# A sliding-window attention block on one core: E by V in tiles of 64 by 32, five equal score sets, masks by VectorE, layer norm as multiply and add

## The chip, the cores and the metric

The kernel runs on one core of one Trainium2 chip. The time is device microseconds of one execution: the median of three runs of the kernel before is 323.15 us (322.97 to 323.19).

## The reference

One transformer block over 2048 positions of width 640, in bfloat16. A vector `c` gives six modulation vectors (shift, scale and gate for each half of the block). With `x` of 2048 by 640:

```python
sa, ca, ga, sb, cb, gb = (silu(c) @ w_mod) split in six
h = layernorm(x) * (1 + ca) + sa
q, k, v = h @ wqkv, in 32 heads of 20
p = softmax(q @ k.T / sqrt(20), only keys with 0 <= query - key < 256)
x = x + ga * ((p @ v) @ wo)
h = layernorm(x) * (1 + cb) + sb
x = x + gb * ((sigmoid(h @ w_gate) * (h @ w_up)) @ w_down)
```

Each query sees 256 keys: itself and the 255 before it. The inner width of the second half is 1536.

## The kernel before, in words

The 2048 positions are cut in eight chunks of 256 queries (two blocks of 128). For each chunk `a` the work is: layer norm and modulation (`ln1`), projection to q, k and v (`qkv`), attention in two halves of 16 heads (`attention`, `q` = 0 and 1, called half chunks here), output projection and residual (`outproj`), second layer norm, gated MLP (`mlp`). A chunk's queries need the keys of two blocks before it and of its own two; chunk 0 has no keys before it.

**Order of the work.** `build` only collects operations with their readers, writers and buffers. `PLAN` (line 365) is a list written out beforehand: each number divided by 5 is an operation, and the remainder is the engine that runs it (0 TensorE, 1 ScalarE, 2 VectorE, 3 GpSimd, here POOL as in the profile, 4 SyncE). `schedule` (line 151) walks this list, places tiles in buffers and keeps each engine's order; `emit` (line 262) works out the semaphore waits. Every engine runs its own operations strictly in that order. [...] The chunks overlap: the projections run ahead of attention, and the MLP of earlier chunks fills TensorE between the pieces of attention.

**Scores.** q and k stand transposed in `QT` and `KT`, four heads on the four groups of 32 partitions (20 used). For chunks 1 to 7 a half chunk has four main sets and one ends set. A main set (`main_set`, line 1052) is 24 matmuls in tiles of 32 rows by 64 columns, eight at once: keys in groups of 64, over the pieces of queries that `PIECES` lists (256, 192 and 64 queries). They fill the four banks of `S`; one ScalarE instruction (line 1067) takes the exponential of all 128 x 2048 into a buffer `E`. An ends set (`ends_set`, line 1027) holds the far and near corners of four heads' windows: 32 matmuls of 64 queries in tiles of 32 rows by 128 columns, one exponential (line 1041) into a buffer `G`. POOL then masks with affine selects (lines 1045, 1072, 1076), part of which copy corners from `E` to `G`. Chunk 0 has three sets for each half chunk (`score_set`, line 1082), masked on line 1112.

**E by V.** `burst` (line 1121) makes one operation for each half chunk: 64 matmuls (32 in chunk 0) in tiles of 128 rows by 32 columns. The stationary operand is 128 keys by one head's 20 values, a column of ones for the softmax sum, and padding (heads stand 22 apart in `V`); the moving operand is `E` or `G`, 256 or 128 queries. Four tiles, one for each group of 32 output partitions, work at once, and the sums go to two banks of `M` (two heads side by side in each). In chunks 1 to 7 the burst is glued ahead of the second score set of the next half chunk (`with_pv`, line 1001). Then VectorE transposes, takes the reciprocal of the sums, divides, and transposes again (lines 1162 to 1194).

**V.** For each block of 128 keys two chains of five matmuls (320 columns each, heads 0 to 15 and 16 to 31) go to a bank of `M`; one eviction each, on ScalarE or VectorE as the list says (lines 914, 915), writes `V`. `M` has four banks, which all projections, the MLP and the bursts share.

**Layer norm.** VectorE computes mean and variance (`bn_stats`, `bn_aggr`), POOL adds epsilon and raises to -0.5 (lines 800, 802), and the normalisation is subtract and multiply on VectorE (line 815); for six blocks, fixed in `XHP`, POOL does it as multiply and add (lines 807, 812).

Of the kernel before, what the change touches and what calls it, by code (L numbers as in the profile page):

```python
# [360 lines left out]
def c_pe(n):  # L361
# [133 lines left out]
FILL = 1  # L495
WSE = (("dve", "pool"), ("dve", "pool"))
QMAX = 4.5
NE = 6
EW = 2048
PAIR = 0  # L500
PAIRO = 0
XHP = ((2, 0), (3, 0), (4, 0), (4, 1), (5, 0), (5, 1))
MOE = ("dve", "act", "pool")


# [882 lines left out]
```

## Time and profile before

| | |
|---|---|
| median of three runs | 323.15 us |
| span of the profiled execution (first to last instruction) | 321.8 us |
| matmuls / weight loads | 5045 / 5045 |
| VectorE instructions | 424 |
| ScalarE instructions | 229 |
| POOL instructions | 349 |
| HBM read / written | 18.68 MB / 2.62 MB |

How to read it: the span is that of the one execution that the profiler recorded; what lies around it (323.15 - 321.8 = 1.35 us, launch and end) is part of the measured time and not of the profile. Engines are PE (TensorE matmul), PEld (TensorE weight load, which overlaps PE), DVE (VectorE), ACT (ScalarE), POOL (GpSimd) and SP. All matmuls are recorded by one helper, lines 698 (whole array) and 699 (tiles), so they are told apart by the names of their tiles: `S<-QT,KT` are scores, `M<-E,V` is E by V. A line of the timeline gives start, length, engine, line, operation, output and inputs, shape of the array tile, and the count of instructions merged in it; in brackets stands the idle time before it and what ended that. A line of the groups gives busy time, mean nanoseconds of one, and the idle time before them. A line of the stretches gives busy time and count for PE, PEld, DVE, ACT and POOL, then the granted clock and the share and rate of the DMA engines.

### The profile page before, as it was taken

The numbers are of one execution on the slowest core, as the hardware profiler recorded it, in microseconds if no ns is written. First come the engines' busy times: TensorE is split into PE (matmuls) and PEld (weight loads), VectorE is DVE, ScalarE is ACT, GpSimd is POOL, SyncE is SP. The second block draws the span as 40 slices with busy tenths as digits, with TensorE's granted clock in tenths as the row PEclk, the third lists the DMA queues.
The fourth block names the chain that finished last, engine by engine and source line by source line (L and its number), as shares of the span: only waits on it lengthen the run. The fifth ranks groups of instructions, "written<-read, shape, count | busy, mean of one in ns | idle before, by whom it ended". The sixth has DMA issues, their size and how long they took to land.

```text
span 321.8 us, 11465 instructions
## 1 busy us (share of the span) xinstructions
PE 315.6 (98%) x5045; PEld 236.8 (74%) x5045; DVE 198.8 (62%) x424; ACT 213.9 (66%) x229; POOL 189.5 (59%) x349
## 2 busy tenths in 40 slices
PE   6999999999999999999999999999999999999996
PEld 2677767677877777766777677877877777877885
DVE  4689987877886746584555555465534474386323
ACT  2699997877787986768686867676976746411220
POOL 3338759878768493949484848577575826601000
PEclk9999999999999999999999999999999999999999
DMA  7999999999922534126526100220800004002101
GB/s 249 348 262 278 223 179 248 194 225 295 206 36 43 88 75 55 44 63 108 77 19 111 37 22 2 63 42 25 132 18 4 22 22 104 20 5 61 43 0 41
DMA packets 62123, 32.92 MB, mean 102 GB/s; under 512 B 45946, under 2 KB 60794, under 8 KB 62074
## 3 DMA queue, kind: packets, MB, share of 16 engines
q1 hardware_dynamic: 59904, 29.73, 43.5%
q10 hardware_dynamic: 2170, 2.46, 2.8%
q8 instruction: 39, 0.64, 0.9%
q14 instruction: 10, 0.08, 0.1%
HBM read 18.68 MB, written 2.62 MB: 66 GB/s over the span
## 4 chain that ended last, share of the span: by engine, by line
PE 96%; DMA 1%; DVE 1%; ACT 1%; issue 0%; ACTq 0%
PE M L698 79%; PE S L699 8%; PE M L699 7%; DMA x<-in_A_x_dram 1%; ACT hT L831 1%; DVE st L793 1%; PE S L698 1%; PE S L690 0%; ACT stg L914 0%; ACTq L584 0%; DVE x L815 0%; DVE st L795 0%; ACT hT L914 0%; DVE x L1308 0%; DVE mA L778 0%
## 5 line engine op out<-in xcount | busy, mean ns | idle before, releaser
L1067 ACT ACTIVATE E<-S 128x2048 bf16<-128x2048 f32 x56 | 105.0, 1875 | 40.6 <-PE S L699 40.2
L1072 POOL TENSOR_SCALAR_AFFINE_SELECT E<-E 128x256 bf16<-128x256 bf16 x112 | 46.6, 427 | 57.1 <-ACT E L1067 25.1
L1076 POOL TENSOR_SCALAR_AFFINE_SELECT E<-E 128x512 bf16<-128x512 bf16 x112 | 70.6, 646 | 4.6 <-DVE x L815 1.2
L698 PE MATMUL M<-h2T,wg 128*128 128x256 bf16 x480 | 67.0, 273 | 0.0
L698 PE MATMUL M<-h2T,wu 128*128 128x256 bf16 x480 | 66.7, 273 | 0.0
L1289 DVE SCALAR_TENSOR_TENSOR hh<-sig,M 128x512 bf16<-128x512 f32 x48 | 32.4, 678 | 42.9 <-ACT sig L1287 26.4
L698 PE MATMUL M<-wd,hh 128*128 128x320 bf16 (+2 forms) x396 | 57.1, 295 | 0.0
L698 PEld LDWEIGHTS M<-h2T,wg 128*128 128x128 bf16 x480 | 45.4, 98 | 7.8 <-DVE T L1162 0.2
L698 PEld LDWEIGHTS M<-h2T,wu 128*128 128x128 bf16 x480 | 45.2, 98 | 7.3
L1287 ACT ACTIVATE sig<-M 128x512 f32<-128x512 f32 x48 | 28.5, 595 | 31.2 <-PE M L698 30.9
L698 PEld LDWEIGHTS M<-wd,hh 128*128 128x128 bf16 x396 | 37.2, 98 | 13.7 <-DVE hh L1289 0.2
L1045 POOL TENSOR_SCALAR_AFFINE_SELECT E<-E 128x1024 bf16<-128x1024 bf16 x28 | 32.0, 1147 | 4.9 <-ACT E L1041 3.4
L699 PEld LDWEIGHTS S<-QT,KT 20*64 20x64 bf16 (+1 forms) x1856 | 20.0, 100 | 17.4 <-issue 9.7
L699 PE MATMUL S<-QT,KT 20*64 20x256 bf16 (+5 forms) x1856 | 32.3, 228 | 0.4 <-issue 0.4
L1041 ACT ACTIVATE E<-S 128x2048 bf16<-128x2048 f32 x14 | 26.3, 1876 | 6.8 <-PE S L699 6.7
L793 DVE BATCH_NORM_STATS2 st<-x 128x6 f32<-128x320 bf16 x64 | 28.9, 479 | 2.4 <-DMA x<-in_A_x_dram 1.8
L1162 DVE STREAM_TRANSPOSE T<-M 128x512 f32<-128x512 f32 x32 | 21.5, 700 | 12.9 <-PE S L699 11.6
L698 PE MATMUL M<-wk,hT 128*128 128x320 bf16 x160 | 27.9, 299 | 0.0
L1308 DVE TENSOR_TENSOR x<-M,x 128x320 bf16<-128x320 f32 (+2 forms) x33 | 15.4, 475 | 18.8 <-PE M L698 18.6
L698 PE MATMUL M<-wq,hT 128*128 128x320 bf16 x160 | 26.2, 299 | 0.7 <-DVE hT L832 0.5
L698 PE MATMUL M<-wv,hT 128*128 128x320 bf16 x160 | 26.0, 299 | 0.0
L698 PE MATMUL M<-wo,oT 128*128 128x320 bf16 x160 | 25.9, 299 | 0.0
(84 smaller groups left out, 356.4 us busy)
## 6 DMA issues: line engine op xcount, KB each, us to landing
x<-in_A_x_dram SPq DMA_DIRECT2D x18, 160.0 KB, 3.7
wd<-in_w_mod_dram SPq DMA_DIRECT2D x6, 320.0 KB, 5.4
wd<-in_B_w_down_dram SPq DMA_DIRECT2D x4, 480.0 KB, 5.5
wu<-in_w_mod_dram SPq DMA_DIRECT2D x5, 320.0 KB, 4.8
x<-in_A_x_dram ACTq DMA_DIRECT2D x8, 160.0 KB, 2.7
out_dram<-x SPq DMA_DIRECT2D x8, 160.0 KB, 1.9
wu<-in_B_w_up_dram SPq DMA_DIRECT2D x2, 576.0 KB, 4.7
wg<-in_B_w_gate_dram SPq DMA_DIRECT2D x2, 576.0 KB, 6.8
```

The lines of the kernel that those rows point to most:

```text
L698: return e.matmul(o, l, r, start=st, stop=sp, skip_group_check=True)
L699: return e.matmul(o, l, r, start=st, stop=sp, tile_position=tp, skip_group_check=True)
L793: A("dve", lambda e, g, bi=bi, j=j: e.bn_stats(v(bi * 12 + j * 6, 6), src[bi].ap[:, j * 320:(j + 1) * 320]), 0.48, reads=[src[bi].r()], wr ...
L1041: A("act", lambda e, eng: e.activation(cell().rearrange("p m (x c) -> p m x c", c=64)[:, :, 0:4:3, :], Sp.ap[:].rearrange("p j (k x c) -> ...
L1045: A("pool", lambda e, eng, c0=c0, pat=pat, base=base, cm=cm: e.affine_select(cell()[:, :, c0:c0 + 64], cell()[:, :, c0:c0 + 64], pattern=p ...
L1067: A("act", lambda e, eng: e.activation(part(0, 512), Sp.ap[:], ACT.Exp, scale=SM_SCALE), 1.876, reads=[Sp.r()], writes=[E.r("C"), E.r("B") ...
L1072: A("pool", lambda e, eng, hc=hc, src=src, far_h=far_h: e.affine_select(side(hc), part(src, 64), pattern=[[0, 4], [-1 if far_h else 1, 64] ...
L1076: A("pool", lambda e, eng, c0=c0, near=near: e.affine_select(part(c0, 128), part(c0, 128), pattern=[[0, 4], [1 if near else -1, 128]], com ...
L1162: A("dve", lambda e, g, h=h: e.transpose(T1.ap[:, 512 * h:512 * h + 512], X[h].ap), 0.694, reads=[X[h].r()], writes=[T1.r(h)], prio=3.5, t ...
L1287: A("act", lambda e, g, pg=pg, sg=sg: e.activation(sg.ap[:], pg.ap[:], ACT.Tanh, scale=0.5), c_act(512), reads=[pg.r()], writes=[sg.r()], ...
L1289: A("dve", lambda e, g, pu=pu, sg=sg, f0=f0: e.scalar_tensor_tensor(out=hh.ap[:, f0:f0 + 2, :], in0=sg.ap[:].rearrange("p (a b) -> p a b", ...
L1308: A("dve", lambda e, g, ps=ps, bi=bi, c0=c0, n=n: e.tensor_tensor(x1[bi].ap[:, c0:c0 + n], ps.ap[:, 0:n], x1[bi].ap[:, c0:c0 + n], op=ALU. ...
```

## The change

- **Score sets.** All sets of a half chunk have one form: tiles of 32 rows by 64 columns, 512 columns for each tile, eight tiles at once. The two column halves of the array now hold two pairs of heads (before: two groups of 64 keys of the same heads). A group of 64 keys `x` (from -4 to 3, counted from the chunk's start) is scored against the 64, 128, 192 or 256 queries that can see it, so nothing is scored in both an ends set and a main set. Five sets for each half chunk: two of pieces of 256, two of 192, 64, 64, 192, one of 128. The ends set and `G` go. Chunk 0 has two sets for each half chunk and one that both share: five, where it had six.
- **E by V.** Tiles of 64 rows by 32 columns: 64 keys, eight tiles at once. The lower and upper 64 partitions hold different heads and add into different banks of `M`. 128 matmuls for each half chunk (64 in chunk 0); the lengths follow `LENS`.
- **V** is laid out to match: each projection chain of 320 columns takes every other pair of heads from `wv`, and two evictions of 64 partitions each bring it to the partitions of its heads: 64 evictions where there were 32.
- **Masks** are one VectorE minimum each (two from a set of chunk 0's first two) of `E` with a buffer `mk` that holds 0 or 3e38, the row block of `mk` repeated over the groups: 79 of them. `mk` is made once at the start.
- **Layer norm** is multiply and add for all blocks but chunk 0's first norm: POOL computes the negated mean and its product with the inverse deviation (two small operations for each norm), and the list chooses VectorE or POOL for the normalisation.
- `E` has eight buffers where it had six and `G` (the same memory). The order list is a new one, with 1977 operations where it had 2097.

```diff
-NE = 6
+NE = 8
 EW = 2048
+BIG = 3.0e38
...
+            def mki(e, g, p0=p0, c0=c0, op=op):
+                src = p_sig.aps[0][p0:p0 + 64, p0:p0 + 64].bitcast(I32)
+                for i in range(2):
+                    ins = e.tensor_scalar(mk[p0:p0 + 64, c0 + i * 64:c0 + i * 64 + 64], src, 0.0, BIG, op0=op, op1=ALU.mult)
+                return ins
...
+        if not one:
+            A("pool", lambda e, g: e.tensor_scalar(v(34, n), st.ap[:, 24:28].rearrange("p (b t) -> p b t", t=2)[:, :, 0], -1.0, None,
+                                                   op0=ALU.mult), 0.2,
...
+                return e.tensor_scalar(dst[bi].ap[:], src[bi].ap[:], v(30 + bi, 1), v(32 + bi, 1), op0=ALU.mult, op1=ALU.add)
+            A("dve" if one else ("dve", "pool"), xh, {"dve": 0.44, "pool": 0.87}, port=True,
...
+                    ps.ap[:, 0:320].rearrange("p (g c) -> p g c", c=40), hT[a].ap[:, kt, bi * 128:(bi + 1) * 128],
+                    wv[:, kt, :].rearrange("p (g c) -> p g c", c=80)[:, :, 40 * half:40 * half + 40])) for kt in range(NDT)]
...
+                for odd in range(2):
+                    evac(lambda b=b, half=half, odd=odd: heads(V[b].ap[64 * half:64 * half + 64, 352 * odd:352 * odd + 352], VW)[:, :, 0:DH],
+                         lambda ps=ps, odd=odd: heads(ps.ap[64 * odd:64 * odd + 64, 0:320], DH), 320, [ps.r()], [V[b].r((half, odd))], 6.5,
+                         f"evv{a}")
...
+    ONE = ((-1, 0), (0, 256))
+    TWO = ((-2, 0), (-4, 192), (3, 256), (1, 320))
+    SETS = (([(h, x, c) for x, c in st] for st in (ONE, TWO) for h in range(2)))
+    SETS = [list(x) for x in SETS] + [[(h, x, c + 256 * h) for h in range(2) for x, c in ((-3, 0), (2, 128))]]
+    MASKS = [(192, 512, 4, 128, 64)] * 2 + [(128, 512, 4, 256, 0)] * 2 + [(64, 256, 8, 128, 64)]
+    FIRST = ((1, 0), (3, 192), (0, 256))
...
+                v = E.ap.rearrange("p (g c) -> p g c", c=step)[:, :, c0:c0 + w]
+                return e.tensor_tensor(v, v, mk[:, m0:m0 + w].unsqueeze(1).to_broadcast([128, g, w]), op=ALU.min)
...
+    XS = {64: (-4, 3), 128: (-3, 2), 192: (-2, 1), 256: (-1, 0)}
+    LENS = (64, 256, 192, 192, 128, 128, 192, 256, 128, 128, 192, 256, 256, 64, 64, 64)
+    LENS0 = (64, 192, 256, 256, 128, 128, 192, 64)
...
+                ins = mm(e, X[half].ap[32 * j:32 * j + 32, h * 256 + q0:h * 256 + q0 + n],
+                         V[2 * a + kb].ap[64 * half:64 * half + 64, v0:v0 + 32],
+                         E.ap[64 * half:64 * half + 64, j * 512 + c:j * 512 + c + n], t not in seen, True, tp=(64 * half, 32 * j))
```

A helper, `run`, issues the matmuls of a set or a burst: it goes round the eight tiles and always takes the one whose columns so far are fewest.

More of the change, by code (lines that the diff above doesn't have):

```diff
@@ L1001, in with_pv @@
+    last = {"s": fills, "p": []}
     def with_pv(name, sc, dur, rd, tiles, before, mode):
         if before is None:
-            return A("pe", sc, dur, reads=list(rd), writes=[tiles[-1].r()], prio=10, lat=0.2, tag=name, extra=last["s"], mode=mode,
-                     hold=tiles[:-1])
+            return A("pe", sc, dur, reads=list(rd), writes=[t.r() for t in tiles[1:]], prio=10, lat=0.2, tag=name, extra=last["s"], mode=mode,
+                     hold=tiles[:1])
         pa, pv, pd, prd, X = before
@@ L1011, in with_pv @@
         rd.update(prd)
-        return A("pe", both_of, pd + 0.09 + dur, reads=list(rd), writes=[tiles[-1].r(), X[0].r(), X[1].r()], prio=10, lat=0.2,
-                 tag=f"pvs{pa}", extra=last["s"], mode=2, mout=mode, hold=tiles[:-1] + X)
+        return A("pe", both_of, pd + 0.09 + dur, reads=list(rd), writes=[t.r() for t in tiles[1:]] + [X[0].r(), X[1].r()], prio=10, lat=0.2,
+                 tag=f"pvs{pa}", extra=last["s"], mode=4, mout=mode, hold=tiles[:1] + X)
     def keys_of(a, kb, lo, gi, j, n):
@@ L1020, in set_reads @@
         rd = {}
-        for kb in range(-2, 2):
+        for kb in range(-2 if a else 0, 2):
             rd[KT[(2 * a + kb) // 2].r((kb % 2, q))] = 1
@@ L1121, in burst, with run @@
-    def burst(a, q, sets, Es, G):
+    def run(e, prog, emit):
+        at = {t: p[0] for t, p in prog.items()}
+        pos = dict.fromkeys(prog, 1)
+        ins = None
+        while pos:
+            t = min(pos, key=lambda t: (at[t], list(prog).index(t)))
+            what = prog[t][pos[t]]
+            if isinstance(what, int):
+                at[t] = max(at[t], what)
+            else:
+                ins = emit(e, t, what)
+                at[t] += what[-1]
+            pos[t] += 1
+            if pos[t] == len(prog[t]):
+                del pos[t]
+        return ins
@@ new lines, in score_set, with put, fn @@
+    def score_set(a, name, parts, masks, before):
+        E, Sp = Tile(p_E, f"E{a}_{name}"), Tile(p_S, f"S{a}_{name}")
+        def sc(e, eng):
+            prog = {(j, half): [0] + [(q, h, x, c, piece(x)[3]) for q, h, x, c in parts] for j in range(4) for half in range(2)}
+            def put(e, t, what):
+                j, half = t
+                q, h, x, c, n = what
+                kb, odd, q0, n = piece(x)
+                gi = 4 * q + 2 * half + h
+                return mm(e, Sp.ap[64 * half:64 * half + 64, j, c:c + n], keys_of(a, kb, 64 * odd, gi, j, 64),
+                          QT[a].ap[32 * j:32 * j + DH, gi, q0:q0 + n], True, True, tp=(32 * j, 64 * half))
+            return run(e, prog, put)
+        rd = {}
+        for q in dict.fromkeys(x[0] for x in parts):
+            rd.update(set_reads(a, q))
+        last["s"] = [with_pv(f"score{a}", sc, 0.262, rd, [E, Sp], before, 3)]
+        A("act", lambda e, eng: e.activation(E.ap.rearrange("p (j c) -> p j c", j=4), Sp.ap[:], ACT.Exp, scale=SM_SCALE), 1.876,
+          reads=[Sp.r()], writes=[E.r()], prio=3, tag=f"exp{a}")
+        for c0, step, g, w, m0 in masks:
+            def fn(e, eng, c0=c0, step=step, g=g, w=w, m0=m0):
+                v = E.ap.rearrange("p (g c) -> p g c", c=step)[:, :, c0:c0 + w]
+                return e.tensor_tensor(v, v, mk[:, m0:m0 + w].unsqueeze(1).to_broadcast([128, g, w]), op=ALU.min)
+            A("dve", fn, c_dve(g * w, 2.0), port=True, reads=[E.r(), R_mk], writes=[E.r()], prio=5, tag=f"mask{a}")
+        for q, h, x, c in parts:
+            where[a, q, h, x] = E, c
+        return E
@@ L1123, in burst @@
+    XS = {64: (-4, 3), 128: (-3, 2), 192: (-2, 1), 256: (-1, 0)}
+    LENS = (64, 256, 192, 192, 128, 128, 192, 256, 128, 128, 192, 256, 256, 64, 64, 64)
+    LENS0 = (64, 192, 256, 256, 128, 128, 192, 64)
+    where = {}
+    def burst(a, q):
         X = [Tile(p_M, f"O{a}_{q}x"), Tile(p_M, f"O{a}_{q}y")]
         X[0].mate, X[1].mate = X[1], X[0]
+        of = {n: [(h, x) for h in range(2) for x in XS[n] if a or x >= 0] for n in XS}
+        mine = [p + where[(a, q) + p] for p in (of[n].pop(0) for n in (LENS if a else LENS0))]
@@ L1139, in pv @@
-            for (E, _), st in zip(Es, sets) if not a else ():
-                for k, kb, u, n, cu in st[0]:
-                    bank = k // 2
-                    oc = (k % 2) * 256 + u * 128
-                    for j in range(4):
-                        h = 16 * q + 4 * j + k
-                        ins = mm(e, X[bank].ap[32 * j:32 * j + 32, oc:oc + n * 128], V[2 * a + kb].ap[:, h * VW:h * VW + 32],
-                                 E.ap[:, j * 512 + cu * 128:j * 512 + (cu + n) * 128], (bank, j) not in seen, True, tp=(0, 32 * j))
-                        seen.add((bank, j))
@@ L1154, in burst @@
+            return run(e, prog, put)
+        rd = {x[2].r(): 1 for x in mine}
         for kb in range(-2 if a else 0, 2):
-            rd[V[2 * a + kb].r(0)] = 1
-            rd[V[2 * a + kb].r(1)] = 1
-        return a, pv, (6 if a else 3) * 512 / 2400.0 * 1.04 + 0.02, rd, X
+            for half in range(2):
+                for odd in range(2):
+                    rd[V[2 * a + kb].r((half, odd))] = 1
+        return a, pv, 1.165 if a else 0.6, rd, X
     def norm(X, Tn, q, a):
@@ L1172, in build, with later @@
     pend = []
-    def later(a, q, sets, Es, G, close):
+    def later(a, q, close):
         made = []
         def first():
-            made.append(burst(a, q, sets, Es, G))
+            made.append(burst(a, q))
             return made[0]
@@ L1183, in alone @@
         pa, pv, pd, prd, X = first()
-        A("pe", pv, pd, reads=list(prd), writes=[X[0].r(), X[1].r()], prio=8, lat=0.2, tag=f"pvs{pa}", mode=2, hold=X, extra=last["s"])
+        A("pe", pv, pd, reads=list(prd), writes=[X[0].r(), X[1].r()], prio=8, lat=0.2, tag=f"pvs{pa}", mode=4, hold=X, extra=last["s"])
         then()
@@ L1215, in attention @@
             if a < NOW:
-                alone(*later(a, q, sets, Es, G, close))
+                alone(*later(a, q, close))
             else:
-                pend.append(later(a, q, sets, Es, G, close))
+                pend.append(later(a, q, close))
     def add_pair(x, pss, prio, tag):
```

195 lines of the change are left out of this document (43 added, 152 removed), and 218 rows, old and new, of the table PLAN.

## The prediction

> **What bounds the kernel now.** I read the page first, then the chain that ended last, then the busy times in stretches of 20 us, then the timeline around one burst, and last the groups by line and shape.
>
> ```profile
> span 321.8 us, 11465 instructions
> PE 315.6 (98%) x5045; PEld 236.8 (74%) x5045; DVE 198.8 (62%) x424; ACT 213.9 (66%) x229; POOL 189.5 (59%) x349
> PEclk9999999999999999999999999999999999999999
> PE 96%; DMA 1%; DVE 1%; ACT 1%; issue 0%; ACTq 0%
> PE M L698 79%; PE S L699 8%; PE M L699 7%; DMA x<-in_A_x_dram 1%; ACT hT L831 1%; DVE st L793 1%; PE S L698 1%; PE S L690 0%; ACT stg L914 0%; ACTq L584 0%; DVE x L815 0%; DVE st L795 0%; ACT hT L914 0%; DVE x L1308 0%; DVE mA L778 0%
> ```
>
> TensorE is the chain: 96% of it, at the full granted clock. No other engine is above 66%. So a microsecond less of TensorE work is a microsecond less of time, as long as nothing else makes it wait. The places where something could are the stretches in which VectorE is nearly full:
>
> ```profile
> 20.00:40.00 20.00, 20.00 (x407) 14.21 (x405) 18.81 (x47) 18.81 (x22) 15.27 (x24) 1.00 1.06 259
> 40.00:60.00 20.00, 19.60 (x332) 13.55 (x331) 16.00 (x39) 16.82 (x21) 15.02 (x28) 1.00 1.15 210
> 60.00:80.00 20.00, 20.00 (x322) 14.66 (x320) 15.45 (x34) 15.68 (x17) 16.14 (x29) 1.00 1.12 246
> 80.00:100.00 20.00, 20.00 (x348) 15.19 (x347) 16.80 (x40) 16.02 (x16) 13.55 (x24) 1.00 0.58 111
> 100.00:120.00 20.00, 20.00 (x348) 15.03 (x347) 12.20 (x26) 16.20 (x20) 14.96 (x28) 1.00 0.42 75
> ```
>
> The columns after the length are PE, PEld, DVE, ACT, POOL. From 20 to 40 us VectorE and ScalarE are each busy 18.81 of 20, and TensorE still loses nothing. From 100 us on VectorE has room: 12.20 of 20.
>
> **The change part by part.**
>
> *The burst (E by V).* Fourteen bursts of 64 matmuls (chunks 1 to 7, two each) and two of 32 (chunk 0). One of the fourteen, with the score set behind it and a later "ends" set:
>
> ```profile
> 189.19 1.30 PEld L699 LDWEIGHTS M<-E,V 128*32 128x32 bf16 x64 [0.30 <-POOL E L1076]
> 190.66 0.27 PEld L699 LDWEIGHTS S<-QT,KT 20*64 20x64 bf16 x24 [0.16 <-issue]
> 191.01 0.11 PEld L698 LDWEIGHTS M<-h2T,wg 128*128 128x128 bf16 x2
> 191.25 1.04 PE L698 MATMUL M<-h2T,wu 128*128 128x256 bf16 x8
> 192.12 0.43 PE L698 MATMUL M<-wo,oT 128*128 128x320 bf16 x2
> 192.39 0.82 PE L698 MATMUL M<-h2T,wg 128*128 128x256 bf16 x6
> 193.05 0.38 PE L698 MATMUL M<-h2T,wu 128*128 128x256 bf16 x2
> 193.36 0.29 PEld L699 LDWEIGHTS S<-QT,KT 20*128 20x128 bf16 x32 [0.21 <-issue]
> 193.70 0.25 PEld L698 LDWEIGHTS M<-wo,oT 128*128 128x128 bf16 x3
> ```
>
> Price of a column: eight matmuls of 256 columns take 192.12 - 191.25 = 0.87, so 0.109 each; two of 320 take 0.27, so 0.135. The difference of 64 columns is 0.026: 0.41 ns a column, and 0.004 us for each matmul beside it. A burst now runs four tiles (128 rows by 32 columns) side by side; each streams 4 x (256 + 128 + 128 + 256) = 3072 columns in 16 matmuls: 3072 x 0.41 ns = 1.26, plus 16 x 0.004 = 0.06. Measured from its first weight load to the next one it is 190.66 - 189.19 = 1.47, so 0.15 is start and drain. After the change eight tiles (64 rows by 32 columns) run side by side, and the pieces of one tile (64, 256, 192, 192, ...) add up to 2560 columns, again in 16 matmuls: 1.05 + 0.06 + 0.15 = 1.26. The columns saved are keys that the mask zeroes anyway. Saved: 0.21, from which I take 0.02 because eight tiles start one after another and not four. 14 x 0.19 = 2.7 us. The bursts are alike, the first and the last in the chain being
>
> ```profile
> 53.16 1.43 PE M L699 x64
> 280.81 1.44 PE M L699 x64
> ```
>
> The trace has no tile of 64 x 32. The nearest row for eight tiles at once is the set at 190.66 (24 matmuls, 512 columns per tile, 0.35 to the next load; 0.21 of it columns); the nearest for short pieces is the ends set at 193.36: 32 matmuls of 64 columns, eight rounds of new weights on four tiles, 512 columns per tile, 0.34 to the next load. Short pieces there cost their columns and no more. So I take full overlap; the ends are 3.0 saved (no stagger) and nothing saved (first rival).
>
> [...]
>
> *The score sets.* Before, a half chunk has four sets like that at 190.66 (0.35) and one ends set (0.34). After, five sets of 512 columns per tile: +0.01 each half chunk, 0.1 in all. Chunk 0 has five sets in place of six: one set less is 0.35 and the change of array shape ahead of it. The matmuls from 193.05 stream until 193.05 + 2 x 0.109 = 193.27, the set begins at 193.36: 0.09. Saved: 0.44. Chunk 0's bursts lose 256 columns per tile each, 2 x 0.105 = 0.2, but the first now has another shape than the matmuls right ahead of it, which costs it that 0.09: 0.1 saved.
>
> ```profile
> 29.25 0.88 PE L699 MATMUL M<-wu,silubc 128*32 128x160 bf16 x40
> 29.95 0.83 PE L699 MATMUL M<-E,V 128*32 128x256 bf16 x32
> ```
>
> TensorE in all: 2.7 + 0.44 + 0.1 - 0.1 = 3.1 us less.
>
> *V's projection* reads wv in eight runs of 40 columns. Nearest rows: a moving operand in five runs of 32 (hh) and one in a single run (wd):
>
> ```profile
> L699 PE MATMUL M<-wd,silubc 128*32 128x160 bf16 x20 | 0.8, 233 | 0.0
> L699 PE MATMUL M<-hh,silubc 128*32 128x160 bf16 x20 | 0.8, 233 | 0.0
> ```
>
> Equal, so nothing. If runs of 40 were to cost a tenth more, 160 x 0.0135 = 2.2 us; no row suggests it.
>
> *Masks.* They leave POOL (149 us in these three groups, and chunk 0's beside them) and come to VectorE as 79 two-input minimums.
>
> ```profile
> L1076 POOL TENSOR_SCALAR_AFFINE_SELECT E<-E 128x512 bf16<-128x512 bf16 x112 | 70.6, 646 | 4.6 <-DVE x L815 1.2
> L1072 POOL TENSOR_SCALAR_AFFINE_SELECT E<-E 128x256 bf16<-128x256 bf16 x112 | 46.6, 427 | 57.1 <-ACT E L1067 25.1 <-DVE Tn L1166 8.4 <-PE S L699 7.5
> L1045 POOL TENSOR_SCALAR_AFFINE_SELECT E<-E 128x1024 bf16<-128x1024 bf16 x28 | 32.0, 1147 | 4.9 <-ACT E L1041 3.4 <-DVE x L815 1.5
> L1333 DVE TENSOR_TENSOR wo<-wo,gbc 128x640 bf16<-128x640 bf16 x5 | 2.1, 486 | 0.0
> L1308 DVE TENSOR_TENSOR x<-M,x 128x320 bf16<-128x320 f32 x31 | 14.8, 485 | 17.3 <-PE M L698 17.1
> L1308 DVE TENSOR_TENSOR x<-M,x 128x128 bf16<-128x128 f32 x1 | 0.3, 292 | 0.2 <-PE M L698 0.2
> ```
>
> With one input in f32 VectorE's two-input operation costs (485 - 292) / 192 = 1.0 ns an element and 164 ns; the all-bf16 row (640 in 486) fits half of that slope, 164 + 640 x 0.5. The masks are all bf16 in SBUF, so I take the half slope: 256, 512 and 1024 elements are 0.29, 0.42 and 0.68. 4 x 0.29 + 32 x 0.42 + 43 x 0.68 = 43.8 us. At the full slope it would be 31 us more; that end is the second rival. Behind a mask on VectorE stand the evictions of M, for whose four buffers TensorE waits; a burst waits for its five masks.
>
> *The rest is moved by the new order list* (a number's remainder by 5 is its engine). VectorE gets 29 evictions of V instead of 23 (+2.9), 28 of q and k instead of 34 (-2.9), 10 normalisations instead of 26 (16 x 0.446 = -7.1), 8 scalings of wo and wd instead of 16 (-4.1), 22 modulations instead of 11 (+3.7), and 1.8 less in small ones: 198.8 + 43.8 - 9.3 = 233 us, 72%. ScalarE gets 35 evictions of V instead of 9 (+11) and 22 modulations instead of 50 (-16): no fuller than now. POOL takes the normalisations, scalings and modulations that VectorE and ScalarE give up, and ends well under half full.
>
> ```profile
> L915 DVE CAST V<-M 128x320 bf16<-128x320 f32 x23 | 10.9, 478 | 7.7 <-PE M L698 7.5
> L914 ACT ACTIVATE V<-M 128x320 bf16<-128x320 f32 x9 | 3.8, 430 | 0.2 <-PE M L698 0.2
> L815 DVE TENSOR_SCALAR x<-x,st 128x640 bf16<-128x640 bf16 x26 | 11.2, 446 | 8.6 <-POOL st L802 8.4
> L840 DVE TENSOR_SCALAR h2T<-h2T,scB,shB 128x256 bf16<-128x256 bf16 x4 | 1.3, 342 | 0.0
> L839 ACT ACTIVATE hT<-hT,mA 128x256 bf16<-128x256 bf16 x23 | 12.6, 591 | 0.0
> 191.20 1.31 DVE L1162 STREAM_TRANSPOSE T<-M 128x512 f32<-128x512 f32 x2 [1.44 <-PE S L699]
> L1162 DVE STREAM_TRANSPOSE T<-M 128x512 f32<-128x512 f32 x32 | 21.5, 700 | 12.9 <-PE S L699 11.6
> ```
>
> An eviction of V now covers 64 partitions and 320 elements; I price it like the full one, between half and the same. [...]
>
> *Does VectorE hold TensorE up?* I summed these mean times over VectorE's entries that stand between the same points of TensorE's work in the two orders, each less the 0.08 or so by which neighbours overlap (two transposes of 0.70 take 1.31 in the rows above). From 20 to 40 us of TensorE work they grow from 18.1 to 19.7, in the next three stretches of 20 us by 1.7, 3.4 and 0.1. On the windows shown that gives 20.4, 17.7, 18.9 and 16.9 of 20. The first is over: 0.4 us is lost if VectorE can be filled fully, 1.7 if no stretch can go above the 18.81 seen. I take 0.6, nearer the low end because TensorE loses nothing in the fullest stretch now.
>
> Sum: 321.8 - 3.1 + 0.6 = 319.3 of span. The median of the runs, 323.15, stands 1.35 above the span of the profiled execution; I keep that: **320.6 us**.
>
> **The rivals.**
>
> *Short pieces cost more on eight tiles.* Two short pieces behind one another leave about 30 ns to load the next weights of eight tiles, and 16 instructions must issue in that time. If a 64-column round costs what a 128-column one does (+0.026), the burst has five of them and the half chunk's two mixed sets two each: 9 x 0.026 x 14 = 3.3, and the time is 323.9 (half of it: 322.2). For it: no row has short pieces on eight tiles. Against it: the ends set.
>
> *VectorE becomes the bound (slower).* If the masks, whose second input is a repeated row, run at the full slope, chunk 0's nine cost 2.1 more and every later chunk's ten 4.1 more, 3.0 of that in the first stretch after chunk 0's. The four stretches then need 22.5, 20.7, 23.0 and 21.0 of 20: 7.2 us late, against 3.1 saved, so 323.15 + 4.1 = 327.2. It decides from about 0.2 us more per mask: 9 masks in the first stretch and 10 in the third then make it 2.2 and 0.9 late, which is the 3.1 saved. Against it: the bf16 row at half slope.
>
> *Instructions don't come fast enough (slower).*
>
> ```profile
> q8 instruction: 39, 0.64, 0.9%
> ```
>
> Thirty-nine packets for 2 x 5045 TensorE instructions are about 259 each, and a packet takes 0.9% x 16 x 321.8 / 39 = 1.2 us. A burst with its set goes from 176 instructions in 1.8 us to some 304 in 1.6. If a packet is sometimes late by 0.3 us per burst that is 4.2: 324.8. Nothing in the profile shows such a wait now.
>
> *The two row halves don't run at once* (the change then doesn't do what it says): each burst streams 2 x 1.05: +0.9 x 14 = 12.6, 333. The set at 190.66 has four row groups at once, which speaks against it.
>
> **How the numbers follow.** Forecast 0.74 (319.3 to 322.2 by its bounds: stall 0 to 1.7, burst saving down to half); short pieces at their full price 0.10; VectorE 0.09; instructions 0.04; row halves 0.03. About 0.2% (0.65 us) is what a measurement here can tell from no change. Faster: the forecast and a little of the first rival, 0.75. Same: the rest of it, 0.10. Slower: 0.15. The range is 319.2 to 323.5: the forecast with its bounds and half of the first rival.
>
> **What would show it.** Right: bursts of 128 matmuls, about 1.26 from their first weight load to the next one; 75 exponentials; masks of 0.42 and 0.68 on VectorE; VectorE near 233, POOL under 95; TensorE near 312.5 busy; between 20 and 40 us VectorE at 19 or more and TensorE losing under 1 us. Wrong: bursts over 1.4, rounds of 64 columns at 50 ns, masks at 0.68 and 1.19, or TensorE waiting for VectorE by several us before 100 us.

## The result, and the profile after

The changed kernel takes 341.85 us (median of four runs, 340.12 to 343.31) against 323.17 for the kernel before (322.97 to 323.36): a ratio of 1.057, 95% interval 1.052 to 1.062. The forecast was 320.6. The profiled run took 343.28 with a span of 341.3. Single runs of a kernel in which TensorE stands still differ by up to 3%; the ratios leave out a run that is more than 1.5% above the fastest of its kernel, and the single times are given where that matters.

The page of the changed kernel: span, busy times, granted clock, the queue that brings instructions, and the chain that ended last.

```profile
span 341.3 us, 13404 instructions
PE 318.4 (93%) x6069; PEld 234.5 (69%) x6069; DVE 229.8 (67%) x490; ACT 213.9 (63%) x236; POOL 79.9 (23%) x161
PEclk9999999999999999999999999998999999999999
q8 instruction: 47, 0.77, 0.9%
PE 83%; issue 5%; ACT 4%; DVE 3%; DMA 2%; POOL 1%; SPq 1%; POOLq 0%
```

TensorE stands for 341.3 - 318.4 = 22.9 us where it stood for 6.2 before. Nothing else became full: VectorE has 229.8 us (forecast 233), GpSimd 79.9 (under 95). New in the chain is "issue", 5%: time in which TensorE waits for nothing that the profile shows. What TensorE waits for, in us, times and longest:

```profile
PE M L708 <- issue: 8.7, 5, 3.0
PE S L708 <- issue: 5.3, 3, 1.8
PE S L707 <- ACT silubc L678: 1.9, 1, 1.9
PE M L707 <- issue: 1.8, 3, 1.2
```

VectorE comes only behind these, with 1.4 once at the start and 0.3 at a time. Line 708 is the matmul on tiles: bursts and score sets. The chain between 121 and 149 us (start, us, what):

```profile
121.70 3.67 PE M L707 x29
125.37 1.29 PE M L708 x120
126.66 2.46 issue
129.12 0.20 PE M L708
129.32 0.35 PE S L708 x16
...
144.58 1.30 PE M L708 x119
145.88 0.35 PE S L708 x15
146.24 1.80 issue
148.04 0.29 PE S L708
```

A burst runs, and with its last piece, or with the last matmul of the set behind it, TensorE stops for two microseconds. The chain has eight such pieces over half a microsecond: 3.00 at 40.69, 0.99 at 48.91, 1.18 at 76.39, 1.98 at 106.67, the two above, 1.73 at 230.74 and 1.80 at 252.33; 14.9 us together. Other bursts pass freely, which rules out a wait that every burst has. What the stopping places have in common shows when the instructions between them are counted (columns: length, PE, PEld, then the rest):

```profile
108.60:126.60 18.00, 17.95 (x382) 13.05 (x381) 15.20 (x32) 13.34 (x14) 4.07 (x9) 1.00 0.24 53
129.05:146.10 17.05, 16.98 (x381) 12.88 (x381) 11.73 (x25) 14.64 (x16) 1.89 (x3) 1.00 0.40 64
147.95:230.60 82.65, 82.35 (x1784) 60.30 (x1784) 58.88 (x115) 62.56 (x61) 11.57 (x22) 1.00 0.37 61
232.40:252.30 19.90, 19.83 (x382) 14.36 (x382) 10.93 (x22) 11.67 (x9) 2.99 (x6) 0.91 0.15 35
```

Matmuls and weight loads from one standstill to the next are 763, 762, 3568 and 764. With the few instructions that the page doesn't count these are 768, 768, 3584 and 768: 3, 3, 14 and 3 times 256. In the compiled list of TensorE's instructions all eight standstills fall at positions that leave the same remainder by 256, within one. The queue called "instruction" moves 0.77 MB in 47 packets of 16 KB; for the 2 x 6069 matmuls and loads of the page that is 258 each, and with the multiples above I take a packet as a block of 256 instructions. One of them lies in the standstill at 126.66; this is the DMA view from 126.5 to 128.0 (40 slices of 0.0375 us, then the queue's packets, MB and share of 16 engines):

```profile
GB/s 0 0 0 0 0 0 0 0 437 0 0 0 0 0 0 0 0 0 0 0 0 0 0 0 0 0 0 0 0 0 0 0 0 0 0 0 27 89 102 205
q8 instruction: 1, 0.02, 3.8%
```

It begins in the ninth slice, at 126.8, and takes 3.8% x 16 x 1.5 = 0.9 us. The timeline around it:

```profile
125.30 1.36 PE L708 MATMUL M<-E,V 64*32 64x64 bf16 x127
129.12 0.20 PE L708 MATMUL M<-E,V 64*32 64x64 bf16 x1 [2.46 <-issue]
```

TensorE goes on 1.4 us after the packet has landed. Before that it had used up a block in 1.3 us: 127 matmuls and their loads, 254 instructions. So I read: TensorE has the block that it works on and at most the next one; the next but one is as a rule fetched only after a block end is passed. By the compiled list 41 of the 47 packets start after TensorE has entered the block ahead, up to 4.5 us after, and six before it, by up to 1.4; none lands less than 1.2 us before TensorE begins the block that follows. From one block end to the next usable block it took 3.3 to 7.1 us at the eight standstills.

Not every burst in which a block lies nearly whole stands still. By the compiled list there are eight such bursts in chunks 1 to 7: five stand for 1.7 to 2.5 us, the last for 0.35, and those at 212.65 and 272.69 pass. The packets of the trace tell them apart. All eight standstills listed above end 1.4 to 1.5 us after a packet of this queue has landed, but the packet does not always start at the same point: it starts 1.9 us after TensorE enters the block ahead at 125 us, 0.7 after it at 211, and 1.4 before it at 272. Why it starts earlier or later is not shown.

After the standstill at 230.74 the granted clock falls as well: 0.91 in the stretch from 220 to 240. By the trace's clock record it is half (0.50) for 3.41 us from 233.26 on, which is 1.7 us lost.

A burst without a standstill, by its weight loads:

```profile
89.87 1.26 PEld L708 LDWEIGHTS M<-E,V 64*32 64x32 bf16 x128 [0.27 <-issue]
91.17 0.16 PEld L708 LDWEIGHTS S<-QT,KT 20*64 20x64 bf16 x16
91.52 0.33 PEld L707 LDWEIGHTS M<-h2T,wu 128*128 128x128 bf16 x4 [0.20 <-issue]
```

It takes 91.17 - 89.87 = 1.30 to the next load, where 1.47 was before and 1.26 was forecast.

### The profile page after: what moved, and what is told of

Same layout as the page of the kernel before. It is cut to its first block, busy times and chain, and to the rows that moved or that the text cites. A ratio compares the mean times of both kernels' runs of the same rounds, so it can differ in the third digit from the quotient of the medians.

```text
span 341.3 us, 13404 instructions
## 1 busy us (share of the span) xinstructions
PE 318.4 (93%) x6069; PEld 234.5 (69%) x6069; DVE 229.8 (67%) x490; ACT 213.9 (63%) x236; POOL 79.9 (23%) x161
## 4 chain that ended last, share of the span: by engine, by line
PE 83%; issue 5%; ACT 4%; DVE 3%; DMA 2%; POOL 1%; SPq 1%; POOLq 0%
PE M L707 69%; PE S L708 7%; PE M L708 6%; DMA x<-in_A_x_dram 2%; ACT E L1070 2%; SPq L582 1%; ACT V L923 1%; DVE V L924 1%; POOL mk L602 1%; POOL x L824 1%; DVE E L1075 1%; PE S L707 0%; POOL hT L849 0%; DVE st L802 0%; SPq L831 0%
## 5 line engine op out<-in xcount | busy, mean ns | idle before, releaser
L1070 ACT ACTIVATE E<-S 128x2048 bf16<-128x2048 f32 x75 | 140.7, 1876 | 55.2 <-PE S L708 54.8
L707 PE MATMUL M<-h2T,wg 128*128 128x256 bf16 x480 | 69.6, 276 | 0.0
L707 PE MATMUL M<-wd,hh 128*128 128x320 bf16 (+2 forms) x396 | 60.5, 297 | 0.4 <-issue 0.4
L707 PEld LDWEIGHTS M<-h2T,wg 128*128 128x128 bf16 x480 | 46.6, 99 | 9.6 <-issue 1.2
L1075 DVE TENSOR_TENSOR E<-E,mk 128x1024 bf16<-128x1024 bf16 (+2 forms) x79 | 43.4, 562 | 9.2 <-ACT E L1070 8.0
L708 PE MATMUL S<-QT,KT 20*64 20x64 bf16 (+3 forms) x1920 | 33.4, 236 | 5.8 <-issue 5.3
L708 PEld LDWEIGHTS S<-QT,KT 20*64 20x64 bf16 x1920 | 17.4, 104 | 21.7 <-issue 11.6
L708 PE MATMUL M<-E,V 64*32 64x64 bf16 (+3 forms) x1920 | 21.5, 231 | 7.4 <-issue 7.4
L708 PEld LDWEIGHTS M<-E,V 64*32 64x32 bf16 x1920 | 19.2, 90 | 11.5 <-issue 9.7
L849 POOL TENSOR_SCALAR h2T<-h2T,scB,shB 128x256 bf16<-128x256 bf16 x17 | 9.4, 555 | 73.3 <-DVE E L1075 22.7
L1260 DVE TENSOR_TENSOR x<-M,x 128x320 bf16<-128x320 f32 (+2 forms) x33 | 15.5, 471 | 16.2 <-PE M L707 15.8
```

The source lines that it names most:

```text
L707: return e.matmul(o, l, r, start=st, stop=sp, skip_group_check=True)
L708: return e.matmul(o, l, r, start=st, stop=sp, tile_position=tp, skip_group_check=True)
L849: return e.tensor_scalar(ap, ap, sc[:, dt:dt + 1], sh[:, dt:dt + 1], op0=ALU.mult, op1=ALU.add)
L1070: A("act", lambda e, eng: e.activation(E.ap.rearrange("p (j c) -> p j c", j=4), Sp.ap[:], ACT.Exp, scale=SM_SCALE), 1.876, reads=[Sp.r()], ...
L1075: return e.tensor_tensor(v, v, mk[:, m0:m0 + w].unsqueeze(1).to_broadcast([128, g, w]), op=ALU.min)
L1260: A("dve", lambda e, g, ps=ps, bi=bi, c0=c0, n=n: e.tensor_tensor(x1[bi].ap[:, c0:c0 + n], ps.ap[:, 0:n], x1[bi].ap[:, c0:c0 + n], op=ALU. ...
```

## The experiments

Theory A: instructions come in blocks of 256, one ahead, and a burst with its set (some 290 instructions in 1.65 us) uses a block up faster than the next one comes, if a block lies nearly whole within it. Rival B: the 64x32 tile or its two row halves are slow by themselves. Rival C: the masks on VectorE make TensorE wait.

**Half the instructions on the same tiles.**

```
prog = {(half, j): [0] + [(i % 2, x[1], x[2], 192, 320) for i, x in enumerate(mine[::2])] ...}   # a > 0
```

> The changed kernel, but each burst of chunks 1 to 7 runs 64 matmuls of 320 columns in place of 128 of 64 to 256: the same eight tiles of 64x32 at once and the same 2560 columns for each tile, with half the instructions (which keys and queries meet is no longer the reference's, so the attention is another one; chunk 0, sets, masks and order are as they were). Theory A, TensorE's instructions are not fetched fast enough: the standstills in the bursts of chunks 1 to 7 (11.0 us) go, perhaps also the one at 76 us (1.4) and the drop of the clock after 230 us (1.6), the one of chunk 0 stays (3.2): 326 to 331 us, and bursts of about 1.3 us. Rival B, the tile of 64x32 or its two row halves are slow by themselves: 338 or more. Rival C, the masks on VectorE make TensorE wait: 338 or more, since the masks are the same.

Measured: 328.06 us (before in the same set of runs: 324.01; ratio 1.011, 1.008 to 1.014). TensorE's largest wait for "issue", and one burst in the timeline:

```profile
PE M L708 <- issue: 3.0, 2, 2.3
```

```profile
88.96 0.94 PEld L708 LDWEIGHTS M<-E,V 64*32 64x32 bf16 x64 [0.26 <-issue]
90.17 0.16 PEld L708 LDWEIGHTS S<-QT,KT 20*64 20x64 bf16 x16 [0.27 <-issue]
```

As theory A had it: no burst of chunks 1 to 7 stands still, and 13.8 us of the 18.7 are gone with the tile, the row halves, the masks and the order unchanged. B and C fall. The burst takes 1.21; twice as many, shorter pieces cost 0.09 of the 1.30.

**The same work with the block ends moved.** Some full matmuls are cut in two column parts, so that the ends fall in the middle of the bursts (first kernel) or just behind their start (second).

```
+ if 0 < k < len(pairs) - 1 and PADS and PADS[0] > 0:
+     PADS[0] -= 1
+     mm(e, o[:, 0:u], l, r[:, 0:u], False, False)
+     ins = mm(e, o[:, u:], l, r[:, u:], False, False)
+     continue
```

> The changed kernel with 310 of its full matmuls cut in two column parts, so many ahead of each burst that the ends of TensorE's 256-instruction blocks fall about 180 instructions after the start of each burst of chunks 1 to 7 (145 for one). Same result, same columns; each cut costs about 4 ns, 1.3 us in all. Theory A: no standstill in those bursts (the changed kernel had none where the end fell 83 to 227 instructions after the start), so 341.9 - 11.0 + 1.3 = 332, and less where the standstill at 76 us, those of chunk 0 and the drop of the clock go too: 326 to 333 us. Rivals B (tile shape) and C (masks on VectorE): 341 to 344, since nothing of theirs is changed.

> The changed kernel with 460 of its full matmuls cut in two in the same manner, but so that the block ends fall 29 or 30 instructions after the start of eleven bursts, and 251, 102 and 76 after that of three. Theory A: about 2.05 us of standstill in ten of those bursts, 2.6 at 251, 0.5 in the last burst and at 76: 24 us in place of 11.0, and 1.9 for the cuts: about 355 us (350 to 360), 22 more than the kernel with its block ends at 180. Rivals B and C: the same as that kernel, within 1 us.

Measured: 331.64 and 362.52 us (the second 360.01, 362.25, 362.79 and 365.95), 31 us apart. What TensorE waits for, first in the kernel with the ends in mid-burst, then in the other:

```profile
PE M L710 <- issue: 2.7, 2, 1.8
PE M L711 <- issue: 0.7, 1, 0.7
```

```profile
PE S L711 <- issue: 19.4, 11, 2.8
PE M L710 <- issue: 3.0, 2, 2.4
PE M L711 <- issue: 3.0, 2, 2.3
```

The two kernels do the same arithmetic and differ only in which matmuls are cut and how many (310, and 385, not the 460 of the expectation). From the sixth burst on even the cuts are the same: 75 more of them ahead of it move the ends, and of the eleven bursts there all stand still in the second kernel, ten of them for 1.5 to 2.8 us, and none in the first. (In an earlier burst the first kernel still stands for 0.7, at 56.15; and the changed kernel did have a standstill with the end at 227, the one at 106.67.) This is theory A's strongest evidence: the place of the block end alone makes or takes some 20 us of standstill. The 355 that I expected for the second left out the clock. Two stretches behind the standstill at 109.14 (1.95 us):

```profile
108.00:112.00 4.00, 2.05 (x114) 1.51 (x98) 1.49 (x3) 0.60 (x1) 2.07 (x5) 1.00 0.02 4
112.00:116.00 4.00, 4.00 (x61) 3.35 (x59) 3.29 (x7) 2.37 (x4) 1.73 (x3) 0.57 0.02 4
```

From 112 to 116 the clock is 0.57. Six of the stretches of 20 us have 0.91, each with 3.41 us at half clock: some 10 us lost.

**The kernel before with the same appetite.** Each piece of its bursts is cut in two; tiles, masks and order stay as they were.

```
- ins = mm(e, X[bank].ap[32 * j:32 * j + 32, oc:oc + n], ..., src, ...)
+ for y, j in ((y, j) for y in (0, n // 2) for j in range(4)):
+     ins = mm(e, X[bank].ap[32 * j:32 * j + 32, oc + y:oc + y + n // 2], ..., src[:, y:y + n // 2], ...)
```

> The kernel before with every piece of its bursts cut in two: 128 matmuls for a burst on the old tiles of 128x32, the same columns, masks left on GpSimd, the old order; nothing else of the change. Same result. Theory A: a burst and its set are 304 instructions in about 1.8 us, so standstills come where a block end falls early in the burst: counted as in the changed kernel, about 2.1 us in three of the fourteen bursts (ends at 248, 12 and 24 instructions), 0.4 in two (70 and 75), none in the others: 323.2 + 7.2 and up to 0.06 a burst for more matmuls, 330 to 334 us. Rivals B and C: 323 to 327 us with no standstill (64 more matmuls a burst at 4 ns are 3.6 us at most).

Measured: 339.14 us (before 324.01; ratio 1.044, 1.038 to 1.050). Waits, and a burst that passed in the timeline:

```profile
PE S L699 <- issue: 4.7, 3, 2.5
PE M L698 <- issue: 2.8, 2, 2.3
PE M L699 <- issue: 1.8, 1, 1.8
```

```profile
93.05 1.37 PEld L699 LDWEIGHTS M<-E,V 128*32 128x32 bf16 x128 [0.21 <-issue]
94.53 0.27 PEld L699 LDWEIGHTS S<-QT,KT 20*64 20x64 bf16 x24
```

The old kernel stands still as well, with nothing of the change but the number of instructions. The three bursts named beforehand did stand still. A burst that passes takes 1.48, as before (1.47), so the price is not in the pieces themselves. Too small was my sum: one standstill more (2.3 at 77.0, at a block end in full matmuls early in the kernel) and again the clock, low in four stretches of 20 us (0.94, 0.98, 0.91 and 0.91; 5 us).

**Only a shift.** The warm-up matmuls are cut into shorter ones, so that the whole program moves against the blocks: by 124 instructions, and by a whole block as a control.

> The changed kernel with its eleven warm-up matmuls of 512 columns cut into 73 of 73 and 170: the same columns before the real work begins, and 124 instructions more ahead of everything. Nothing else differs, the result is the same. Theory A (instruction fetch in blocks of 256, one block ahead): all block ends move 124 instructions to the front of the work. The five bursts of the changed kernel that stand still from 106 us to 254 us no longer do; instead those whose block end falls 20 and 48 instructions after their start (near 71 and 89 us) and the one at 254 (near 170 us) do. With a refill of 5.0 us before 80 us and 3.6 after, summing over the changed kernel's own times gives 9.0 us of standstill in place of 16.1: 333 to 337 us. Rivals B (tile shape) and C (masks on VectorE): as the changed kernel, 340 to 344 us, with the same places.

> The same with 139 warm-up matmuls of 39 and 56 columns: 256 instructions more, one whole block. Theory A: every block end falls where it fell in the changed kernel, so the same standstills at the same instructions, and the same time within 1.5 us: 340 to 344. If the length of the program or the cut warm-up itself mattered, it would go along with the kernel of 124.

```
- ins = e.matmul(p_S.aps[0][:, 3, :], Eall[:, 0:128], Eall[:, 128:640], ...)          # 2 and 1 of them
+ ins = e.matmul(p_S.aps[0][:, 3, 0:w], Eall[:, 0:128], Eall[:, 128:128 + w], ...)    # 14 and 3, or 26 and 9
```

The control takes 340.37 us (338.32, 338.74, 341.99 and 346.72). Its longest pieces of "issue" after 100 us are 1.62 at 141.72, 1.59 at 209.46, 1.58 at 228.02 and 1.37 at 247.79, all at the changed kernel's block ends. Three of the four are at bursts that stood still there too; the one at 209 is new, and those near 106 and 126 us shrank to 0.38 and to nothing. So the places where TensorE can stand still come from the block ends; whether it does, and for how long, varies by 2 us and more between two executions. The burst that stood for 2.46 at 126 us passes in the control, where its packet starts 2.0 us before TensorE enters the block ahead and not 1.9 after. The shift by 124 met the places, but the time decides nothing: 337.62 us in one run, just over the expected range, and 343.84, 345.61 and 345.81 in the others, no gain. From the chain of the run of 343.84:

```profile
56.41 3.43 issue
...
77.85 2.96 issue
...
100.39 1.19 issue
```

and after 101 us only one over half a microsecond, 1.88 at 183.20. The five late standstills are gone and the three that I had named have come: 2.96 with the end at 20, 1.88 with the end at 254, and 1.19 just behind the burst with the end at 48 and its set. But 3.43 at 56.41, in a burst with its end at 201, and 1.10 at 46.01 were not among them. TensorE waits 11.2 us for "issue" in all where I had 9.0, and half clock follows three of the standstills (0.58 from 60 to 64 us, 0.65 from 81 to 85, 0.82 from 183 to 188), another 5 us. A refill in the first 80 us can take longer than the 5.0 that I had put in: 7.0 ahead of the standstill at 46.01. My sum tells where TensorE can stand, and not how long.

**Masks cut to 8 columns.**

> The changed kernel with every mask on VectorE cut to 8 columns (the attention is then not masked): some 38 us less work on VectorE in front of the bursts, with the same instructions and order on TensorE. Theory A: the standstills stay, 339 to 343 us. Rival C (TensorE waits for the masks): 322 to 332 us.

Measured: 340.69 us (336.77, 337.98, 343.39 and 347.65; the control above, with whole masks, 338.32 to 346.72). VectorE does 30.6 us less: 199.2 busy, with masks of 157 ns. (I had expected 38 less.) TensorE still stands 11.0 us at block ends:

```profile
PE M L708 <- issue: 6.2, 5, 2.4
PE S L708 <- issue: 4.4, 5, 1.4
PE M L707 <- issue: 0.4, 2, 0.3
```

The control stands 11.7 us so. Against its three lower runs (338.32 to 341.99) the two lower ones here are 0.3 to 5.2 us less, and both are below the 339 that I expected at the least. The masks may cost a few microseconds and not 18: rival C falls a second time.

**The kernel before, shifted.**

> The kernel before with its warm-up matmuls cut so that 126 instructions more stand ahead of everything; nothing else differs, the result is the same. Theory A: a block end now falls 19 to 30 instructions after the start of four of its bursts of 64 matmuls, but a burst with its set is only 176 instructions, so a block lasts over 4 us wherever it ends: no standstill, 323 to 325 us. If cutting the warm-up or the place of the block ends cost time by itself, 326 or more.

Measured: 323.27 us against 323.48; ratio 0.9997 (0.9976 to 1.0018). Four of its bursts now have a block end 19 to 30 instructions after their start, where the changed kernel stands for 2 us, and nothing happens. With 176 instructions a burst and its set can't swallow a block.

**The best that the real work can have, and the change without its standstills.**

> The changed kernel with 192 instructions more in the warm-up and 150 of its full matmuls cut in two column parts, chosen by the same sum so that no block is used up faster than it is refilled where that can be had: block ends 139 to 210 instructions after the start of the bursts of chunks 1 to 7 (100 in one). Same result. Theory A: 2.6 us of standstill are left, in chunk 0 and near 55 us, in place of 16.1, and the cuts cost 0.7: 325 to 329 us. Rivals B and C: 340 to 344. If A holds and this still isn't under the 324.0 of the kernel before, the change had little to give even without the standstills.

> The changed kernel with long pieces in every burst, chunk 0's too: 32 matmuls of 320 columns there, 64 in the other bursts, on the same tiles with the same columns for each tile (other keys meet other queries, and chunk 0's masks are cut to 8 columns, so the attention is not the reference's). Theory A: against the kernel with long pieces in chunks 1 to 7 only (328.1), the standstill of chunk 0 (2.4) and the half clock after it (1.9) go, those near 26 and 75 us (0.9 and 1.0) may stay: 322 to 325 us, which is what the change is worth without its standstills. If bursts of 64 matmuls still stood still where a block end falls 25 to 46 instructions after their start (three of them here), 330.

Measured: 332.93 us (329.44, 331.61, 334.24 and 334.74) for the block ends placed by my sum (with 214 cuts, not 150), and 327.45 for long pieces everywhere (before: 323.90 and 323.48). The first is over its range: it has a standstill of 2.0 left in chunk 0 and two of 0.4, and 6.8 us of half clock behind the first (mean clock of the run 0.99). The second is over my range too, for a reason that I hadn't on my list. Its standstill in the bursts of chunk 0 is gone, and instead the timeline shows:

```profile
45.26 0.49 DVE L1287 TENSOR_TENSOR wo<-wo,gbc 128x640 bf16<-128x640 bf16 x1 [2.70 <-DMA wo<-in_A_wo_dram]
45.67 1.31 DVE L1120 STREAM_TRANSPOSE T<-M 128x512 f32<-128x512 f32 x2
46.44 1.51 PE L707 MATMUL M<-wv,hT 128*128 128x320 bf16 x5 [2.41 <-DVE T L1120]
```

VectorE waits 2.7 us for the load of wo, its transposes wait behind that, and TensorE waits for the buffers that they empty. In the changed kernel the same wait (2.81, until 43.79) lies under the standstill of 40.69 to 43.69 and can't be seen. One number of the order list gives that scaling to GpSimd:

```
-    ... 1130, 1576, 1332, 2991, ...
+    ... 1130, 1576, 1333, 2991, ...
```

> The kernel with long pieces in every burst, with one number of the order list changed: the scaling of wo's third tile, which made VectorE wait 2.7 us for wo's load at 42.6 us with the transposes of chunk 0 behind it, goes from VectorE to GpSimd. If that wait is what still holds TensorE in chunk 0 once the bursts no longer stand still, 2.4 us and the half clock behind it go: 322.5 to 325.5 us. If the load itself or something else is late, 327 or more, as without the move.

> The kernel with the block ends placed (192 instructions in the warm-up, 150 cuts; 332.9) with the same move of wo's third scaling to GpSimd; same result. Its standstill in chunk 0 begins at 41.7 us and ends 1.3 us after a block of instructions has landed, so theory A says that the fetch ends last there and the move gives at most 1 us: 331 to 333. If VectorE's wait ends last there, 329 to 330.

Measured: 326.54 and 331.35 us (before 324.24; ratios 1.011, 1.005 to 1.016, and 1.024, 1.019 to 1.029). The first is 0.9 less, within the spread of the runs; the second has the ratio that it had without the move (1.024), as theory A said. In the first, TensorE's wait for the transposes is gone; GpSimd now waits 3.34 us for wo and nothing behind it is late. But the next load is late at once, TensorE's own:

```profile
46.36 0.25 PE L708 MATMUL M<-wd,silubc 128*32 128x160 bf16 x4 [1.39 <-DMA wd<-in_w_mod_dram]
```

So the wait was real, and it was not the only one: I expected 322.5 to 325.5 and missed. With it moved and long pieces (the attention is not the reference's), the times of TensorE in two stretches are

```profile
20.00:80.00 60.00, 55.73 (x1095) 37.16 (x1094) 51.50 (x118) 52.59 (x63) 33.93 (x57) 1.00 1.03 208
80.00:300.00 220.00, 219.50 (x3651) 161.57 (x3651) 157.00 (x319) 147.29 (x146) 37.67 (x70) 1.00 0.33 61
```

After 80 us it loses 0.5 us; between 20 and 80 us it loses 4.3, where the kernel before lost 0.4. No version that computes the reference came below the kernel before.

## Why the prediction was wrong, point by point

*What failed: the price and the chance of the rival "Instructions don't come fast enough".* Its mechanism was the right one and its rows stood in the prediction (259 instructions a packet, 1.2 us a packet, 304 instructions in 1.6 us). I priced it at 0.3 us a burst and gave it 0.04 because "nothing in the profile shows such a wait now". That was misread: the waits of the kernel before have one,

```profile
PE S L699 <- issue: 0.4, 1, 0.4
```

at 42.46 us in a score set, at the same remainder by 256, and it ends 1.4 us after a packet has landed. Two things more were missing. The 1.2 us is the time of the packet and not that of the refill, which by the standstills is over 3 us (3.3 to 7.1) from one block end to the next usable block, while a burst's 256 instructions, 128 loads and 128 matmuls, pass in 1.30 us, 5 ns each. And 304 is more than 256: a whole block can fall inside a burst with its set, while in the kernel before (176) that can't happen, so that its nearly clean profile is no evidence about the new one. At about 2 us for five of the bursts within which a block lies nearly whole, it was the largest term of the sum: 14.9 us with the standstills in other places, and 1.7 of clock behind one of them. Of the signs of being wrong that the prediction lists, none came: it had no sign for this.

*The burst saving.* 0.19 was forecast for each, with 0.02 taken off for eight starts, an estimate of mine that no run shows by itself; 1.47 - 1.30 = 0.17 was measured in most bursts that pass, 2.4 us in fourteen. The tile of 64x32 does what it promised (1.21 with long pieces, both row halves at once), and the first rival was true at about a third of its price in the burst: 1.30 is 0.04 over the 1.26, where it had 5 x 0.026 = 0.13. 128 matmuls on eight tiles in 1.30 us are 10 ns each, about what they were in the ends set of the kernel before (32 in 0.34). The price of the fourth rival was summed too low: a second 1.05 us of streaming in each burst is 14.7 over the forecast, so 335 and not 333; nothing hangs on it.

*TensorE's busy time.* 312.5 forecast, 318.4 measured. Of the difference 1.7 is half clock; some of it is the modelled end of the last matmul ahead of each standstill; I did not take the rest apart. The kernel with long pieces and wo moved has 313.4, 2.2 under the 315.6 of before.

*Masks, VectorE, GpSimd.* Right. 0.42 and 0.68 were forecast for the masks:

```profile
L1075 DVE TENSOR_TENSOR E<-E,mk 128x1024 bf16<-128x1024 bf16 x43 | 28.9, 683 | 5.3 <-ACT E L1070 5.2
L1075 DVE TENSOR_TENSOR E<-E,mk 128x512 bf16<-128x512 bf16 x32 | 13.8, 435 | 3.0 <-ACT E L1070 2.9
```

The half slope for all-bf16 operands held with a repeated row as well, (683 - 435) / 512 = 0.48 ns an element, and "VectorE becomes the bound" fell.

*The first 80 us.* I allowed 0.6 us there, for VectorE being full, and for nothing else. The last run with long pieces, without standstills in the bursts, loses 3.9 us more between 20 and 80 us than the kernel before, and in one run 2.4, in the other 1.4 of such a loss is waiting for the load of wo or wd. That TensorE would lose under 1 us between 20 and 40 us was right (19.36 busy of 20); that VectorE would be busy 19 or more there was not (18.35). Whether the loads are late because of the new order or were as late before, with other work in front of those who need them, no run settles; I moved one scaling only.

*The sum in hindsight.* 19.5 us more span: 16.7 more standing, of which 15.4 is "issue" (15.8 against 0.4), and 2.8 more busy, of which 1.7 is clock.

## What to carry to other kernels

Count instructions, not only columns: when many small matmuls run side by side, ask how many stand in a burst, how long the burst lasts, and whether a whole block of 256 fits into it, for then the block must be refilled within that time: here a burst used up 256 instructions in 1.30 us, and at the standstills the refill took 3.3 us and more. Here a trace that shows next to no such wait (0.4 us) at 176 instructions said nothing about 290. If TensorE stops with no releaser, count the matmuls and loads from stop to stop: multiples of one number, here 256, give it away, and moving the block ends by cutting a few matmuls elsewhere tests it without touching the suspect; and a standstill can hide another wait, which takes its place when it is gone.

## What the runs showed of the hardware that I had not expected

- TensorE's instructions came in packets of 16 KB, 47 for 12138 counted matmuls and loads, and the five standstills from 106.67 us on lie 768, 768, 3584 and 768 instructions apart, multiples of 256. That they are fetched one block ahead is my reading of the packets' times and of the runs with the block ends moved (331.64 and 362.52 us). With DMA traffic low (after 120 us; a DMA share of 0.02 to 0.40 in these four stretches) TensorE went on 3.3 to 4.2 us after the block end before; in the first 60 us, with the DMA share near 1, it took up to 7.1 (36.59 to 43.69 in the changed kernel, by the starts of its matmuls, at a share of 1.04). Of these 7.1 us 4.5 pass before the packet starts, 1.2 are the packet, and 1.4 what follows its landing. That the traffic is the reason is argued, not tried.
- A standstill of 1.7 to 3 us can be followed by a stretch at half clock, and needn't be. In the changed kernel 1.73 at 230.74 was (0.50 from 233.3 to 236.6), 3.00 at 40.69 was not (1.00 from 43.7 to 60). In the kernel with the block ends just behind the bursts' start 1.95 at 109.14 was (0.57 from 112 to 116), 1.83 at 91.46 was not (1.00 from 88 to 104). In the changed kernel's clock record the fall at 233.26 and the return at 236.67 come 228.69 and 232.11 us after its first entry, at 4.57: 67 and 68 times 3.413. Counted from there in steps of that length, the 1.73 ahead of the fall lies in one step, while the 3.00 at 40.69 falls into two with 1.42 and 1.57, and none of the other six has more than 1.69 in one. That is one fall in one trace; what decides whether the clock falls is not shown.
- 128 weight loads and 128 matmuls on eight tiles take 1.30 us at the least (up to 1.39 where they pass); with 64 and the same columns it is 1.21. On four tiles the same number of instructions (1.48) costs no more than half of it (1.47).
